# Attention by head quads with block transposes and 64-row tiles, and an MoE over mapped blocks with resident weights

## The chip, the cores and the metric

The kernel runs on one core of a Trainium2 chip. The core has five engines that run side by side: TensorE (PE; its weight loads are listed as PEld), VectorE (DVE), ScalarE (ACT), GpSimd (POOL) and SyncE (SP). DMA queues are started from SP, ACT and POOL. The metric is device time in microseconds (us), from the first instruction to the last with what lies around them; smaller is better. Operands lie in SBUF (128 partitions), TensorE's results in PSUM.

## The reference

```python
# q, k, v: [B=8, H=8, S=576, D=64] f32
scores = q @ k.T / 8 - slope[h] * |i - j|       # slope[h] = 2 ** -(h + 1)
scores = where(0 <= i - j < 128, scores, -1e9)
x = (softmax(scores) @ v).transpose(0, 2, 1, 3).reshape(4608, 512)

y_dense = relu(x @ w1_dense) @ w2_dense         # 512 -> 512 -> 512
logits = x @ w_gate                             # 8 experts
e = argmax(logits, 1); g = softmax(logits)[e]
y_moe[t] = g[t] * (relu(x[t] @ w1[e[t]]) @ w2[e[t]])
out = y_dense + y_moe                           # [4608, 512] f32
```

A row of queries sees at most 128 keys, so a tile of 128 keys meets 256 queries: its own 128 and the next.

## The kernel before, in words

The order of the instructions on each engine is set at compile time by a scheduler that also places the semaphores; the program's order is its guide, and pools with a fixed number of buffers limit how far work runs ahead.

**Start.** The buffer of rows for the MoE, `xs_dram` (8 experts x 1024 slots x 512 bf16), is filled with zeros by 16 DMAs of 512 KB (L147), and a list of gates and token numbers, `meta_dram`, is initialised (L139).

**Attention**, `process_batch` (L336), once per batch, all 8 heads together. q, k (SP's queue) and v (ACT's) come in tiles of 128 rows with runs of 256 bytes. TensorE transposes q and k by head pairs in f32 (L374, L380); ACT copies them out (L385, L391, L397), q into two halves that POOL has filled with zeros (L365, L366), so that one matmul over 128 rows serves two heads. v is split into a bf16 high and low part on DVE (L410, L413). `score_key_tile` takes 4 heads and 128 keys: QK matmuls in f32r (a reduced f32 that runs at one column a cycle here) with K=128 (L438, L455), a matmul that adds the mask (L445, L462), the exponential on ACT (L470), a cast to bf16 `phi` on ACT (L475) and the rest `plo` on DVE (L479). Per query tile and head, 3 matmuls for each of two key tiles give the weighted sum and the row sum (L520). DVE copies it out of PSUM (L529, L532), normalises it (L534, L536) and casts it (L545); TensorE transposes it (L556), ACT copies that (L561).

**Gate**, `gate_group` and `gate_block` (L319, L182), five blocks of tokens per batch: the logits in f32 (L322), then about 25 small DVE operations for each block, with a running total that each block takes from the one before. Two indirect scatters on POOL per block bring the row to its expert's next slot (L301) and gate and token number to `meta_dram` (L312).

**MoE**, from L579: 32 pairs of 128-row blocks, 8 blocks per expert whatever their fill. The weights of an expert come in f32 and are cast on ACT (L607 to L617); the rows come through transposing DMAs (L621); the token numbers through L626 and a cast on DVE (L633). Hidden layers dense and expert (L638, L650: 16 matmuls of 256 columns each), relu on ACT (L646, L658), second layers (L663, L674: 512 columns), DVE adds them with the gate (L671, L682), and POOL scatters the 128 rows to the output (L690); slots without a token have a number out of bounds.

Of the kernel before, what the change touches and what calls it, by code (L numbers as in the profile page):

```python
# [22 lines left out]
def kernel(  # L23
# [44 lines left out]

# [27 lines left out]
    nc.vector.tensor_copy(out=pidx_f, in_=pidx_i)  # L96

    d_i = consts.tile([P, PW], I32, name="d_i")
    nc.gpsimd.iota(d_i, pattern=[[1, PW]], base=0, channel_multiplier=-1)
    d_f = consts.tile([P, PW], F32, name="d_f")  # L100
    nc.vector.tensor_copy(out=d_f, in_=d_i)
    inv = consts.tile([P, PW], F32, name="inv")
    inv2 = consts.tile([P, PW], F32, name="inv2")
    nc.vector.tensor_single_scalar(out=inv, in_=d_f, scalar=0.0, op=ALU.is_lt)
    nc.vector.tensor_single_scalar(
        out=inv2, in_=d_f, scalar=float(WINDOW - 1), op=ALU.is_gt
    )
    nc.vector.tensor_tensor(out=inv, in0=inv, in1=inv2, op=ALU.add)
    big = consts.tile([P, PW], F32, name="big")
    nc.vector.tensor_scalar_mul(out=big, in0=inv, scalar1=NEG_BIG)  # L110
    maskbP = []
    mb_f = consts.tile([P, PW], F32, name="mbf")
    for pi in range(NHP):
        mbp = consts.tile([P, 2, PW], BF16, name=f"mbp{pi}")
        for hh in range(2):
            h = 2 * pi + hh
# [611 lines left out]
```

## Time and profile before

| what | value |
|---|---|
| median of 3 runs | 842.09 us (839.64 to 844.87) |
| profiled execution: span from first to last instruction | 840.9 us |
| busy share PE / DVE / ACT / POOL | 72% / 45% / 40% / 24% |
| mean granted TensorE clock | 0.81 |
| 0 to 85 us | constants, zero fill, first loads |
| 85 to 530 us | attention and gate |
| 530 to 564 us | last gate, scatters, first loads of the MoE |
| 564 to 841 us | MoE, 32 pairs of blocks |

The profile lists the busy time of the engines, the idle time before each group of instructions with the event that ended it, and the time in which DMAs land. The granted clock is the share of 2.4 GHz at which TensorE was let run. The four stages are cut by the trace: the last attention matmul (L520) starts at 529.9 us, the first MoE matmul (L638) at 564.2 us. No time around the span is listed; the median of the runs is 1.2 us more than the span.

### The profile page before, as it was taken

Reading aid. Unit: us, or ns where it says so; the run is one execution under the profiler, and the core shown is the slowest. Engines: PE = TensorE matmul, PEld = TensorE weight load, DVE = VectorE, ACT = ScalarE, POOL = GpSimd, SP = SyncE. Lnnn points to the kernel's source line nnn. Section 1 sums busy time; section 2 is a strip of 40 time slices with the busy share of each in tenths; the row PEclk is TensorE's granted clock in tenths of the full one; section 3 lists DMA queues with packets and bytes.
Section 4 is the critical chain, followed back from the end, with each engine's and each line's share of the span. In section 5 each row is a group of like instructions: output and inputs, shape, how many; then the busy total and the mean of one; then the engine's idle time right before and its main releaser. Section 6 shows DMA issues by size and latency. Waiting matters only on the chain. (4 is left out here: it accounts for less than half of the span.)

```text
span 840.9 us, 12351 instructions
## 1 busy us (share of the span) xinstructions
PE 605.5 (72%) x4478; PEld 401.2 (48%) x4520; DVE 374.6 (45%) x1432; ACT 335.4 (40%) x499; POOL 201.8 (24%) x340
## 2 busy tenths in 40 slices
PE   0047948958857868777778678419798878979894
PEld 0035536545435546456357356216556545555562
DVE  7006545646636547638528635503243323333342
ACT  0037129239138148156166276402423414333221
POOL 6000323322231232332130310121222222222122
PEclk9987558559659568668568587659989999999998
DMA  9999025125125026124233034823536444322320
GB/s 73 265 258 145 13 64 104 24 71 124 28 54 117 22 63 117 47 59 94 64 72 65 20 110 156 258 42 83 145 86 157 136 97 128 95 62 69 88 59 32
DMA packets 190973, 79.14 MB, mean 94 GB/s; under 512 B 170047, under 2 KB 178239, under 8 KB 190912
## 3 DMA queue, kind: packets, MB, share of 16 engines
q1 hardware_dynamic: 136240, 41.06, 25.5%
q10 hardware_dynamic: 46480, 23.07, 10.9%
q0 software_dynamic: 8192, 14.22, 5.2%
q8 instruction: 36, 0.59, 0.4%
q14 instruction: 25, 0.20, 0.1%
HBM read 47.27 MB, written 29.99 MB: 92 GB/s over the span
## 5 line engine op out<-in xcount | busy, mean ns | idle before, releaser
L479 DVE TENSOR_TENSOR plo<-p,phi 128x1024 bf16<-128x1024 f32 (+2 forms) x80 | 79.7, 1005 | 126.8 <-ACT phi L475 125.9
L690 POOL DMA_INDIRECT out_dram<-yout,tok_i x64 | 63.0, 985 | 215.6 <-DVE yout L682 89.1
L520 PE MATMUL ax<-vxh,phi 128*128 128x72 bf16 (+1 forms) x576 | 95.8, 224 | 14.6 <-DVE xsav L532 11.5
L520 PE MATMUL ax<-vxh,plo 128*128 128x72 bf16 (+1 forms) x576 | 93.0, 221 | 12.1 <-DVE plo L479 12.1
L520 PEld LDWEIGHTS <-phi 128*128 128x128 bf16 (+2 forms) x1152 | 81.3, 115 | 33.0 <-DVE xsav L532 13.4
L520 PE MATMUL ax<-vxl,phi 128*128 128x72 bf16 (+1 forms) x576 | 94.2, 221 | 0.0
L646 ACT ACTIVATE hdr<-hd 128x1024 bf16<-128x1024 f32 x32 | 32.7, 1023 | 152.2 <-PE hd L638 152.2
L663 PE MATMUL yd<-w2d,hdr 128*128 128x512 bf16 x241 | 66.4, 392 | 30.7 <-DVE ydsb L671 30.2
L638 PE MATMUL hd<-xst,w1d 128*128 128x256 bf16 x512 | 67.8, 278 | 19.8 <-DMA xst<-xs_dram 19.5
L633 DVE CAST tok_i<-meta 128x2 int32<-128x2 f32 x32 | 5.4, 169 | 167.5 <-DMA out_dram<-yout,tok_i 141.6
L470 ACT ACTIVATE p<-sq 128x1024 f32<-128x1024 f32 (+2 forms) x80 | 67.5, 853 | 20.1 <-PE sq L462 11.7
L520 PEld LDWEIGHTS <-plo 128*128 128x128 bf16 (+1 forms) x576 | 68.1, 120 | 15.2 <-DVE plo L479 14.2
L301 POOL DMA_INDIRECT xs_dram<-xnb,slot_i x40 | 39.5, 988 | 144.3 <-DVE onehot L207 104.9
L475 ACT CAST phi<-p 128x1024 bf16<-128x1024 f32 (+2 forms) x80 | 69.4, 879 | 1.5
L638 PEld LDWEIGHTS <-w1d 128*128 128x128 bf16 x512 | 51.0, 100 | 39.1 <-issue 20.6
L674 PE MATMUL ym<-w2e,hmr 128*128 128x512 bf16 x244 | 67.0, 391 | 1.9 <-ACT hmr L658 0.7
L374 PE MATMUL trq<-ident_f,qf 128*128 128x128 f32 (+1 forms) x160 | 36.4, 371 | 37.1 <-ACT qT L391 25.7
L650 PE MATMUL hm<-xst,w1e 128*128 128x256 bf16 x512 | 61.1, 273 | 0.0
L438 PE MATMUL sq<-qT,kT 128*128 128x512 f32 x96 | 57.1, 648 | 4.7 <-ACT p L470 4.4
L312 POOL DMA_INDIRECT meta_dram<-meta,slot_i x40 | 40.6, 1016 | 77.7 <-DMA meta_dram<-meta,slot_i 45.7
L322 PE MATMUL lt<-xtg,wg_sb 128*8 128x64 f32 (+1 forms) x128 | 52.5, 583 | 3.7 <-ACT xtg L561 3.7
L663 PEld LDWEIGHTS <-hdr 128*128 128x128 bf16 x256 | 25.6, 100 | 58.7 <-issue 37.0
(104 smaller groups left out, 1075.2 us busy)
## 6 DMA issues: line engine op xcount, KB each, us to landing
vf<-in_v_dram ACTq DMA_DIRECT2D x32, 256.0 KB, 3.1
qf<-in_q_dram SPq DMA_DIRECT2D x32, 256.0 KB, 6.3
kf<-in_k_dram SPq DMA_DIRECT2D x32, 256.0 KB, 6.3
w2e_f<-in_moe_w_dram ACTq DMA_DIRECT2D x8, 1024.0 KB, 9.1
w1e_f<-in_moe_w_dram SPq DMA_DIRECT2D x8, 1024.0 KB, 6.7
xs_dram<-zinit ACTq DMA_DIRECT2D x8, 512.0 KB, 9.2
xs_dram<-zinit SPq DMA_DIRECT2D x8, 512.0 KB, 10.8
vf<-in_v_dram ACTq DMA_DIRECT2D x8, 128.0 KB, 5.5
```

The source lines that it names most:

```text
L312: nc.gpsimd.indirect_dma_start(out=meta_dram[:, :], out_offset=bass.IndirectOffsetOnAxis(ap=slot_i[:rows, 0:1], axis=0), in_=meta[:rows, : ...
L322: nc.tensor.matmul(out=lt[:E, :ncols], lhsT=wg_sb[:, ds, :], rhs=xtgrp[:, ds, :ncols], start=(ds == 0), stop=(ds == 3),)
L438: nc.tensor.matmul(out=o_ap, lhsT=kT[:, pi, q0 : q0 + krows], rhs=qT[:, pi, :, q0 : q0 + nq], start=True, stop=False,)
L470: nc.scalar.activation(out=p32[:krows, :, :nq], in_=sq_v[:krows, :, :nq], func=ACT.Exp,)
L475: nc.scalar.copy(out=phi[:krows, hq * 4 : hq * 4 + 4, :nq], in_=p32[:krows, :, :nq],)
L479: nc.vector.tensor_tensor(out=plo[:krows, hq * 4 : hq * 4 + 4, :nq], in0=p32[:krows, :, :nq], in1=phi[:krows, hq * 4 : hq * 4 + 4, :nq], o ...
L520: nc.tensor.matmul(out=ax_slice(h), lhsT=lt_, rhs=rt_, start=(imm == 0), stop=(imm == nmm - 1),)
L638: nc.tensor.matmul(out=hd[:, fc, :], lhsT=w1d[:, kc, fc * P : (fc + 1) * P], rhs=xst[:, kc, :], start=(kc == 0), stop=(kc == 3),)
L650: nc.tensor.matmul(out=hm[:, fc, :], lhsT=w1e[:, kc, fc * P : (fc + 1) * P], rhs=xst[:, kc, :], start=(kc == 0), stop=(kc == 3),)
L663: nc.tensor.matmul(out=yd, lhsT=hdr[:, fc, bi * P : (bi + 1) * P], rhs=w2d[:, fc, :], start=(fc == 0), stop=(fc == 3),)
L674: nc.tensor.matmul(out=ym, lhsT=hmr[:, fc, bi * P : (bi + 1) * P], rhs=w2e[:, fc, :], start=(fc == 0), stop=(fc == 3),)
L690: nc.gpsimd.indirect_dma_start(out=out[:, :], out_offset=bass.IndirectOffsetOnAxis(ap=tok_i[:, bi : bi + 1], axis=0), in_=yout[:, :], in_o ...
```

## The change

The whole kernel is written anew around the same arithmetic (high and low bf16 parts of p and v, f32r for QK, f32 for the logits).

**Attention** works in 16 units of 4 heads, with 5 key tiles each, in one software order (`steps`): scores of step n, attend of step n-2. `load_unit` (L125) brings q and k by one POOL DMA each, [128 partitions, 18 rows x 64] in runs of 4608 bytes. `prep_qk` (L143) has DVE transpose 32x32 blocks, one instruction for q and one for k, and then 16 SBUF-to-SBUF DMAs on SP put the pieces in place. Head pairs lie in 64-row halves, so the QK matmuls have K=64 (L275) and the two halves write two PSUM banks; no zeros are needed. The mask goes first (L266). `phi` is no longer cast: it is the upper half of each f32 of `p32`, read with a stride. `attend` has 24 matmuls of 64 or 65 columns; the normalisation reads PSUM (L330, L332); POOL casts the row (L342). v's high part is made on ACT, its low part on POOL.

**Gate**, `gate(b)` (L371), once per batch for all five blocks: the logits in four column tiles of TensorE, one matmul that adds them, 13 DVE operations, ranks of all blocks from matmuls that accumulate, five scatters of rows that carry gate and token number behind the 512 values (L456).

**Weights**: all 18 matrices are cast to bf16 by POOL's DMA while attention runs (L76) and stay in SBUF.

**MoE**: a table made on DVE (L513 to L589) maps 43 blocks (36 full ones, and up to 7 that the experts' remainders need) to experts. Per block: POOL gathers 128 rows (L602) and makes the token numbers (L611); 4 transposes (L621) and a DVE copy (L625); hidden layers with the weights as the moving operand, 512 columns (L630, L638), the expert's address from a register that TensorE loads (L593); relu on ACT with the gate as its scale (L646, L647); 8 transposes (L651), two DVE copies (L655, L656); dense and expert second layers accumulate in one bank (L659, L667); ACT copies it out (L675); POOL scatters it (L676).

```diff
+            nc.gpsimd.dma_start(
+                out=w_all[:, e, wi, :, :],
+                in_=src.rearrange("(ks p) f -> p ks f", p=P),
+            )
...
-        eng.dma_start(
-            out=xs_dram[zi * 4 * P : (zi + 1) * 4 * P, :].rearrange(
-                "(k p) c -> p k c", p=P
-            ),
-            in_=zinit,
-        )
...
-                nc.gpsimd.memset(qT_f[0:D, pi, 1, :], 0.0)
-                nc.gpsimd.memset(qT_f[D:P, pi, 0, :], 0.0)
...
+            nc.gpsimd.dma_start(
+                out=t.rearrange("p r c d -> p (r c d)"),
+                in_=src[b, hs].rearrange("h (p r) d -> (h p) (r d)", r=R),
+            )
...
+        nc.vector.transpose(
+            out=s.rearrange("p c (x r) -> p r c x", r=R),
+            in_=t.bitcast(F32),
...
+                nc.sync.dma_start(
+                    out=d.bitcast(F32)[hh * D + 32 * c : hh * D + 32 * c + 32, pl, 0:S],
+                    in_=s[32 * g : 32 * g + 32, c, :],
+                )
...
+        for r in range(2):
+            nc.tensor.matmul(
+                out=sq[:, r, 0 : 2 * nq],
+                lhsT=ident_b,
+                rhs=mask[:, hq, r, :, 0:nq],
+                start=True,
+                stop=False,
+            )
+        for pl in range(2):
+            for r in range(2):
+                nc.tensor.matmul(
+                    out=sq[:, r, pl * nq : (pl + 1) * nq],
+                    lhsT=kT[r * D : (r + 1) * D, pl, k0 : k0 + P],
+                    rhs=qT[r * D : (r + 1) * D, pl, k0 : k0 + nq],
+                    start=False,
+                    stop=(pl == 1),
+                )
...
-                    nc.scalar.copy(
-                        out=phi[:krows, hq * 4 : hq * 4 + 4, :nq],
-                        in_=p32[:krows, :, :nq],
-                    )
...
+        phi = p32.bitcast(BF16).rearrange("p r l (c t) -> p r l c t", t=2)[:, :, :, :, 1]
+        plo = ppool.tile([P, 2, 2, PW], BF16, name="plo", tag="plo")
+        nc.vector.tensor_tensor(
+            out=plo[:, :, :, 0:nq],
+            in0=p32[:, :, :, 0:nq],
+            in1=phi[:, :, :, 0:nq],
+            op=ALU.subtract,
...
+            n = 0
+            for kj in kl:
+                phi, plo = pbuf[(u, kj)]
...
+                for lhs, rhs, w in (
+                    (hi, vh[:, kj, g, :], D + 1),
+                    (hi, vl[:, kj, g, :], D),
+                    (lo, vh[:, kj, g, :], D + 1),
+                ):
+                    n += 1
+                    nc.tensor.matmul(
+                        out=ax_v[:rows, g, 0:w],
+                        lhsT=lhs,
+                        rhs=rhs,
...
-                nc.vector.tensor_copy(
-                    out=xs[:rows, 0:7, :], in_=ax[:rows, 0, 0 : 7 * VW]
-                )
-                nc.vector.tensor_copy(out=xs[:rows, 7, :], in_=ax[:rows, 1, 0:VW])
...
+        recip = gs.tile([P, 4], F32, name="recip", tag="recip")
+        nc.vector.reciprocal(out=recip[:rows], in_=ax_v[:rows, :, D])
+        xf = xpool.tile([P, 4, D], F32, name="xf", tag="xf", bufs=4)
+        nc.vector.tensor_tensor(
+            out=xf[:rows],
+            in0=ax_v[:rows, :, 0:D],
+            in1=recip[:rows].unsqueeze(2).to_broadcast([rows, 4, D]),
+            op=ALU.mult,
+        )
...
+            for ds in range(4):
+                nc.tensor.matmul(
+                    out=lp[32 * ds : 32 * ds + 32, 0:HF],
+                    lhsT=wg_pad[:, ds, :],
+                    rhs=xT[:, ds, hf * HF : (hf + 1) * HF],
+                    start=True,
+                    stop=True,
+                )
+            nc.scalar.copy(out=lt[:, hf * HF : (hf + 1) * HF], in_=lp[:, 0:HF])
...
+        pc = psum_m.tile([P, NT + 1, E], F32, name="pc", tag="misc")
+        for t in range(NT):
+            nc.tensor.matmul(
+                out=pc[:, t + 1 : NT + 1, :],
+                lhsT=ones_b,
+                rhs=oh[:, t, :].unsqueeze(1).to_broadcast([P, NT - t, E]),
...
+            rows = min(P, S - t * P)
+            ins = nc.gpsimd.indirect_dma_start(
+                out=xs_dram[:, :],
+                out_offset=bass.IndirectOffsetOnAxis(ap=slot[:rows, t : t + 1], axis=0),
+                in_=xrow_i[:rows, t, :],
+                in_offset=None,
...
+    for n in range(len(steps) + LAG):
+        if n < len(steps):
+            u, kj = steps[n]
+            scores(u, kj)
+            if kj == 0 and u + 1 < NU:
+                prep_qk(u + 1, "k")
...
+            if kj == 3 and u + 2 < NU:
+                load_unit(u + 2)
+            if kj == 4:
+                if u % 2 == 0:
+                    load_weights(E if u == 0 else u // 2 - 1)
+                    if u == NU - 2:
+                        load_weights(E - 1)
+        if n >= LAG:
+            u, qi = steps[n - LAG]
+            attend(u, qi)
+            if qi == NT - 1 and u % HQ == HQ - 1:
+                gate(u // HQ)
...
+            er = nc.values_load(
+                er_i[0:1, j : j + 1],
+                engines=[PEE],
...
+            nc.gpsimd.indirect_dma_start(
+                out=xm_i[:, :],
+                out_offset=None,
+                in_=xs_dram[:, :],
+                in_offset=bass.IndirectOffsetOnAxis(ap=row_i[:, j : j + 1], axis=0),
+                bounds_check=NSLOT - 1,
...
+            nc.gpsimd.tensor_tensor(
+                out=tok_i,
+                in0=xm_i[:, TC : TC + 1],
+                in1=inval_i[:, j : j + 1],
+                op=ALU.add,
...
+            for kc in range(4):
+                nc.tensor.matmul(
+                    out=hm,
+                    lhsT=xT[:, kc, :],
+                    rhs=w_all[:, bass.DynSlice(er, 1), 0, kc, :],
+                    start=(kc == 0),
...
+            nc.scalar.activation(out=hr[:, 0, :], in_=hd, func=ACT.Relu)
+            nc.scalar.activation(out=hr[:, 1, :], in_=hm, func=ACT.Relu, scale=gate)
...
+            for c in range(8):
+                nc.tensor.transpose(
+                    out=hps[:, c, :], in_=hr_f[:, c * P : (c + 1) * P], identity=ident_b
+                )
+            hT = mpool.tile([P, 8, P], BF16, name="hT", tag="hT")
+            nc.vector.tensor_copy(out=hT[:, 0:4, :], in_=hps[:, 0:4, :])
+            nc.vector.tensor_copy(out=hT[:, 4:8, :], in_=hps[:, 4:8, :])
...
+            for c in range(4):
+                nc.tensor.matmul(
+                    out=y,
+                    lhsT=hT[:, 4 + c, :],
+                    rhs=w_all[:, bass.DynSlice(er, 1), 1, c, :],
+                    start=False,
```

**DVE at the end of a batch.** Before: the end of the last query tile's chain, and the first block's gate with the second's beginning in it. `lg` is a block's logits, `totals_f` the running count, `rank` a token's place.

```order
L545 CAST xnb<-xnf 64x512
L188 COPY lg<-ltp 128x8
L190 MAX mx<-lg 128x8
L192 TENSOR_SCALAR negmax<-mx 128x1
L207 TENSOR_SCALAR onehot<-lg,mx 128x8
L216 ISA junk,eidx_f<-onehot,evals_f 128x8
L216 ISA eidx_f 128x1
L281 TENSOR_TENSOR totals_f<-totals_f,pt 1x8
L249 ISA junk,rank<-onehot,pc 128x8
L249 ISA rank 128x1
L285 CAST t_i<-totals_f 1x8
L188 COPY lg<-ltp 128x8
```

After: the end of the second unit of a batch. `ks` and `qs` are the transposed k and q of the next unit, `pc` the counts, `basee` the experts' next slots.

```order
L332 TENSOR_TENSOR xf<-ax,recip 64x256
L146 STREAM_TRANSPOSE ks<-kraw 128x18x64
L396 TENSOR_REDUCE mx<-lg 128x5
L399 TENSOR_TENSOR lgs<-lg,mx 128x40
L403 SCALAR_TENSOR_TENSOR cand<-lgs,em_152 128x40
L407 TENSOR_REDUCE e_1312<-cand 128x5
L444 TENSOR_REDUCE se<-ex 128x5
L410 TENSOR_TENSOR oh<-em_152,e_1312 128x40
```

```order
L431 TENSOR_TENSOR sl<-pc,basee 128x40
L437 TENSOR_TENSOR sl<-sl,oh 128x40
L442 TENSOR_TENSOR basee<-basee,pc 128x8
L439 TENSOR_REDUCE slot_f<-sl 128x5
L441 CAST slot<-slot_f 128x5
L146 STREAM_TRANSPOSE qs<-qraw 128x18x64
L291 TENSOR_TENSOR plo<-p_1194 128x1024
```

One chain serves five blocks now, and the next unit's `ks`, `qs` and first `plo` stand around and behind it.

**TensorE and POOL in the MoE.** Before, TensorE goes from the dense hidden layer to the expert's:

```order
L638 LDWEIGHTS w1d
L638 MATMUL hd<-xst,w1d 128x256
L650 LDWEIGHTS w1e
L650 MATMUL hm<-xst,w1e 128x256
L650 LDWEIGHTS w1e
```

After, at the same place (`y` belongs to the block before, `hd` and `hm` to this one):

```order
L667 MATMUL y<-w_all,hT 128x512
L630 LDWEIGHTS xT
L630 MATMUL hd<-w_all,xT 128x512
L638 LDWEIGHTS xT
L593 TENSOR_LOAD er_i
L638 ISA
L638 MATMUL hm<-w_all,xT 128x512
```

and POOL, after (`xr_79` and so on are five buffers for gathered rows):

```order
L676 DMA out_dram<-yo,tok_i 4608x512
L602 DMA xr_79<-xs_dram,row_i 128x260
L611 TENSOR_TENSOR tok_i<-xr_79,inval_i 128x1
L676 DMA out_dram<-yo,tok_i 4608x512
L602 DMA xr_81<-xs_dram,row_i 128x260
```

Before, POOL had the scatter alone. Now a register load stands between the two hidden layers on TensorE, and each of POOL's scatters stands behind a gather and an addition that reads what that gather brings.

**POOL between the second and the sixth unit.** Before, POOL has memsets and the scatters here; after, the loads of weights stand among the loads of q and k and the casts:

```order
L76 DMA w_all<-in_moe_w_dram 128x4x512
L342 CAST xrow<-xf 128x256
L76 DMA w_all<-in_moe_w_dram 128x4x512
L130 DMA kraw<-in_k_dram 128x1152
L342 CAST xrow<-xf 64x256
L76 DMA w_all<-in_moe_w_dram 128x4x512 x2
L130 DMA qraw<-in_q_dram 128x1152
L76 DMA w_all<-in_moe_w_dram 128x4x512
L168 TENSOR_TENSOR vl<-vf_67,vh_69 128x1280
```

All 18 loads of weights stand in the stretch of POOL's order that ends before the sixth unit's loads.

## Rows read from the trace of the kernel before

**Rows 1.** Page, part 1: busy time, share of the span and instructions.

```profile
PE 605.5 (72%) x4478; PEld 401.2 (48%) x4520; DVE 374.6 (45%) x1432; ACT 335.4 (40%) x499; POOL 201.8 (24%) x340
```

**Rows 2.** Stages: stretch, its length, each engine's busy time, granted clock, DMA share, GB/s.

```profile
30.00:85.00 55.00, 27.34 (x205) 18.81 (x206) 13.87 (x21) 23.59 (x32) 0.91 (x6) 0.85 0.97 235
85.00:530.00 445.00, 337.17 (x2720) 226.09 (x2733) 240.98 (x1095) 217.21 (x375) 113.85 (x217) 0.72 0.31 74
530.00:564.00 34.00, 5.25 (x40) 3.62 (x37) 11.35 (x114) 5.67 (x15) 9.46 (x10) 0.55 0.49 128
564.00:841.00 277.00, 233.59 (x1509) 151.23 (x1536) 92.36 (x160) 87.06 (x76) 63.02 (x64) 0.96 0.38 95
```

**Rows 3.** The same stretch, instructions on tile `ax` alone: PE, DVE.

```profile
85.00:530.00 445.00, 103.97 (x1608) 29.34 (x73) 0.72 0.31 74
```

**Rows 4.** Waits, 0 to 110 us: engine, line, releaser, us in total, times, longest.

```profile
ACT qT L391 <- DMA xs_dram<-zinit: 28.5, 1, 28.5
```

**Rows 5.** Waits, 140 to 520 us.

```profile
ACT ex L197 <- DVE negmax L192: 44.3, 30, 5.3
PE pc L227 <- DVE onehot L207: 36.2, 30, 5.3
```

**Rows 6.** Waits of DVE, 564 to 841 us.

```profile
DVE tok_i L633 <- DMA out_dram<-yout,tok_i: 141.6, 26, 8.2
```

**Rows 7.** Groups by line and shape: busy us, mean ns of one, idle before.

```profile
L479 DVE TENSOR_TENSOR plo<-p,phi 128x1024 bf16<-128x1024 f32 x48 | 57.9, 1221 | 121.2 <-ACT phi L475 120.4
...
L479 DVE TENSOR_TENSOR plo<-p,phi 128x768 bf16<-128x768 f32 x16 | 15.2, 948 | 0.8 <-ACT phi L475 0.8
...
L479 DVE TENSOR_TENSOR plo<-p,phi 64x256 bf16<-64x256 f32 x16 | 6.6, 415 | 4.8 <-ACT phi L475 4.6
...
L534 DVE RECIPROCAL recip<-xsav 128x8 f32<-128x8 f32 x32 | 6.2, 195 | 0.3
...
L118 DVE SCALAR_TENSOR_TENSOR mbf<-d_f,big 128x256 f32<-128x256 f32 x8 | 3.4, 422 | 0.2
```

**Rows 8.** Groups by line and shape, the other engines.

```profile
L322 PE MATMUL lt<-xtg,wg_sb 128*8 128x512 f32 x64 | 44.3, 857 | 0.0
...
L561 ACT COPY xtg<-xtp 128x512 f32<-128x512 f32 x32 | 18.7, 585 | 69.5 <-PE xtp L556 69.5
...
L671 DVE COPY ydsb<-yd 128x512 f32<-128x512 f32 x64 | 43.7, 683 | 13.7 <-PE yd L663 10.2 <-PE hm L650 2.9 <-issue 0.2
...
L520 PEld LDWEIGHTS <-phi 128*128 128x128 bf16 x896 | 58.8, 110 | 10.3 <-ACT phi L475 4.9 <-DVE xsav L532 2.3 <-issue 0.5
...
L663 PE MATMUL yd<-w2d,hdr 128*128 128x512 bf16 x241 | 66.4, 392 | 30.7 <-DVE ydsb L671 30.2
```

**Rows 9.** PE's timeline from 318 us: start, length, instruction.

```profile
318.20 0.26 PE L520 MATMUL ax<-vxl,phi 128*128 128x72 bf16 x1
318.26 0.26 PE L520 MATMUL ax<-vxh,plo 128*128 128x72 bf16 x1
...
321.74 0.39 PE L445 MATMUL sq<-mbp,ident_b 128*128 128x512 bf16 x1
321.96 0.20 PE L520 MATMUL ax<-vxh,phi 128*128 128x72 bf16 x1
321.99 0.20 PE L520 MATMUL ax<-vxl,phi 128*128 128x72 bf16 x1
```

**Rows 10.** SP's timeline from 316 us.

```profile
316.40 0.37 SPq L348 DMA_DIRECT2D kf<-in_k_dram  x1
```

**Rows 11.** Page, parts 3 and 6: a queue's packets, MB, share; issues, KB each, landing.

```profile
q0 software_dynamic: 8192, 14.22, 5.2%
...
qf<-in_q_dram SPq DMA_DIRECT2D x32, 256.0 KB, 6.3
...
w1e_f<-in_moe_w_dram SPq DMA_DIRECT2D x8, 1024.0 KB, 6.7
```

**Rows 12.** Line 690, the MoE's scatter, and POOL's timeline from 644 us.

```profile
L690 POOLq MOVE  x64: 29/29/29, 557.7 to 833.4; - x64
...
DMA to landing us min/median/max: 2.1/2.8/6.4
...
645.14 0.98 POOL L690 DMA_INDIRECT out_dram<-yout,tok_i  x1 [3.07 <-DVE yout L682]
648.68 0.98 POOL L690 DMA_INDIRECT out_dram<-yout,tok_i  x1 [2.55 <-DMA out_dram<-yout,tok_i]
...
836.50 0.98 POOL L690 DMA_INDIRECT out_dram<-yout,tok_i  x1 [1.86 <-DMA out_dram<-yout,tok_i]
```

More of the change, by code (lines that the diff above doesn't have):

```diff
@@ L64, with prep_v @@
+    def prep_v(u):
+        vf = vfs[u % 2]
+        vh = vhs[u % 2]
+        vl = qtp.tile([P, NT, 4, D], BF16, name="vl", tag="vl")
+        nc.scalar.copy(out=vh[:, :, :, 0:D], in_=vf)
+        nc.gpsimd.tensor_tensor(out=vl, in0=vf, in1=vh[:, :, :, 0:D], op=ALU.subtract)
+        vparts[u] = (vh, vl)
+    load_unit(0)
     ident_f = consts.tile([P, P], F32, name="ident_f")
@@ L108 @@
[L108 to L116, printed above, removed]
+    tok_c = consts.tile([P, NT], I32, name="tok_c")
+    nc.gpsimd.iota(tok_c, pattern=[[P, NT]], base=0, channel_multiplier=1)
@@ new lines, with gate @@
+    scat_group = "scatters"
+    def gate(b):
+        xT, xrow = cur["xT"], cur["xrow"]
+        lt = lts[0]
+        HF = S // 2
+        for hf in range(2):
+            lp = psum_m.tile([P, 512], F32, name="lp", tag="misc")
+            for ds in range(4):
[5 more added lines that the diff above has]
+                    stop=True,
+                )
+            nc.scalar.copy(out=lt[:, hf * HF : (hf + 1) * HF], in_=lp[:, 0:HF])
+        lg = psum_m.tile([P, NT, E], F32, name="lg", tag="misc")
+        for t in range(NT):
+            nc.tensor.matmul(
+                out=lg[:, t, :],
+                lhsT=lt[:, t * P : (t + 1) * P],
+                rhs=sel,
@@ L576 @@
-        for b in range(B):
-            process_batch(b)
+            tc.declare_no_dep(
+                ins.ins,
+                group=scat_group,
+                reason="every token has a row of its own",
+            )
+            tc.add_to_no_dep_group(scat_group, ins.ins)
+    steps = [(u, kj) for u in range(NU) for kj in range(NT)]
+    prep_qk(0, "q")
+    prep_qk(0, "k")
+    prep_v(0)
+    load_unit(1)
+    LAG = 2
+    for n in range(len(steps) + LAG):
[4 more added lines that the diff above has]
+                prep_qk(u + 1, "k")
+            if kj == 2 and u + 1 < NU:
+                prep_qk(u + 1, "q")
+                prep_v(u + 1)
+            if kj == 3 and u + 2 < NU:
[10 more added lines that the diff above has]
+                gate(u // HQ)
@@ new lines @@
+        nc.vector.tensor_tensor(
+            out=wt[:, 2, 0 : E - 1], in0=n8[:, 1:E], in1=n8[:, 0 : E - 1], op=ALU.subtract
+        )
+        cb = rt.tile([P, E], F32, name="cb")
+        nc.vector.tensor_copy(out=cb, in_=wt[:, 1, :])
+        for e in range(1, E):
+            nc.vector.tensor_tensor(
+                out=cb[:, e : e + 1],
+                in0=cb[:, e - 1 : e],
+                in1=wt[:, 1, e : e + 1],
+                op=ALU.add,
+            )
+        ge = rt.tile([P, NB, E - 1], F32, name="ge")
```

906 lines of the change are left out of this document (369 added, 537 removed).

## The prediction

> **What bounds the kernel now.** I read the page's shares first, then cut the span into stages, then asked in each stage what ends the waits. TensorE is the busiest engine, but only 72% of the span [rows 1], and the stages have different limits [rows 2]. Up to 85 us little computes: ACT stands 28.5 us behind one of the zero-fill DMAs [rows 4], while the DMA engines are 97% busy at 235 GB/s. From 85 to 530 us TensorE is busy 337 of 445 us, at a granted clock of 0.72. The program has 1728 `ax` matmuls (8 batches x 8 heads x 9 pairs of tiles x 3); 1608 of them fall in this stretch [rows 3], 7.44 of 8 batches, so a batch takes 445/7.44 = 59.8 us. Here the engines wait for each other in the gate: ACT 30 times for `negmax`, 44.3 us, and TensorE 30 times for `onehot`, 36.2 us [rows 5], with DVE's many small operations (195 ns for 8 columns, rows 7) in between. From 530 to 564 us nearly nothing is busy: the last gate and its scatters run alone. From 564 to 841 us the clock is 0.96 and TensorE is busy 234 of 277 us; DVE waits 26 times for a scatter to land [rows 6]. A pair of blocks takes 277/32 = 8.65 us.
>
> **The change part by part**, against the profiled execution's 840.9 us of span plus 1.2 us around it.
>
> *Start, 22 us* until the first scores. Removed are the zero fill and the clogged queue. There remain: some 3 us of POOL's memsets; the landing of q and k, 590 KB each, 6.3 us for 256 KB and 6.7 us for 1024 KB [rows 11], taken 9 for two behind each other; two block transposes; SP's 16 copies at 0.37 us an issue [rows 10], 5.9 us, of which q's lie under k's transpose; and 2.1 us to land [rows 12]. 3 + 9 + 2.8 + 5 + 2.1 = 21.9.
>
> *The block transpose* is not in the trace. Nearest is a DVE operation over f32, 1221 ns for 1024 columns [rows 7]; for 1152 columns that is 1.37 us. Twice that, 2.7, is the upper end; below it 0.7, if one operand instead of two halves it. I take 1.4.
>
> *A unit on DVE.* plo 3 x 1.221 + 0.948 + 0.415 = 5.0; five reciprocals and five normalisations of 256 columns, 5 x (0.195 + 0.422) = 3.1 [rows 7]; two transposes 2.8. Sum 10.9. At the unit's end the last attend, both transposes and the first plo of the next unit stand in one chain, and I add half of the transposes and one normalisation, 2.3 us, for what can't overlap: 13.2. The `xsav` copies, the split of v and the casts are gone from DVE; POOL and ACT do what remains of these, one unit ahead, which costs nothing while POOL isn't held up by its loads.
>
> *A unit on TensorE.* A 512-column matmul starts 0.22 us before the next at full clock [rows 9]. Mask and QK are 2048 columns per full key tile, and the five tiles are worth four full ones (3, 0.75 and 0.25): 4 x 4 x 0.22 = 3.5. Attend: 108 matmuls at 0.033 = 3.6 warm (0.06 cold, rows 9). Ten f32 transposes by a quarter of the 857 ns of an f32 matmul of 512 columns [rows 8]: 2.1. Each step goes from 128-row tiles to 64-row tiles and back; a 512-column matmul is listed with 392 ns and its successor starts after 220 [rows 8, 9], so if each change waits for the rest it costs 0.18 us, ten times a unit, 1.8. Sum 11.0. The Trainium skill, "TensorEngine Tiling (Array Packing)", Key Properties, says that changing the tiling mode drains TensorE. By that rule the 1.8 us stand, and without it the total would be 16 x 1.8 = 29 us lower; no run so far shows a change of mode.
>
> *The gate, once a batch.* TensorE's order has it whole before the next unit's scores. Eight f32 matmuls of 288 columns by the 857 ns row, 3.9; ACT's copy 0.3 [rows 8]; five DVE operations at 0.2 up to `oh`, 1.0; small matmuls 1.1: 6.3 us of chain. The other eight operations run under the next scores.
>
> *A batch, 35 us.* By DVE 2 x 13.2 + 6.3 = 32.7. By TensorE 2 x 11.0 / 0.72 + 5 = 35.6, if the clock stays at 0.72. I take 35, since the waits of the one are not all covered by the other; ends 31 (DVE's 10.9 with half the tail, and the gate) and 42 (transposes at 2.7 and the gate at 9). 8 x 35 = 280.
>
> *The weights, 35 us.* 18 loads of 1 MB at the 235 GB/s that the start reached [rows 2] take 18 x 4.5 = 81 us. All stand in POOL's order ahead of the sixth unit's loads; of the units computed meanwhile four are loaded among them, each 1.77 MB of q, k and v and 1.18 MB of copies, 12.6 us at the same rate, so 131 us of DMA meet the compute of five units, 5 x 17.5 = 87 us. The difference is 44; I take 35, since the weights begin before the first unit is done; ends 0 (the engines move both at once) and 75 (the loads come at half the rate when they share it). ACT's weight casts and their waits in the MoE are gone.
>
> *From the last gate to the MoE, 21 us* (34 before, rows 2): gate 6.3, slots 1, five issues of 1.0, landing 2.8 [rows 12], the first gather 3.5, transposes and copy 1.5, first register load 1. The table on DVE, about 30 small operations of 0.2 us, lies beside the scatters. Ends 18 and 30.
>
> *A block of the MoE, 5.5 us.* TensorE: 16 matmuls at 0.22 = 3.5, twelve transposes of 128 columns at a quarter of that = 0.7; relu on ACT 0.585 and a DVE copy of up to 0.683 [rows 8] stand between, partly under the next block's `hd`: 4.9. POOL: the gather's reader starts 3.54 us after it, as 648.68 after 645.14 [rows 12]; with `tok_i` 0.17 and the scatter's 0.98 a cycle is 4.7, and if the scatter also waits for ACT's copy and one more issue is in the way, 6.3. I take 5.5, the middle of POOL's ends. 43 x 5.5 = 236.5, against 277 now for 32 pairs; ends 4.9 and 6.3, 211 and 271.
>
> *Tail* 4.4 us, as now from the last scatter's start at 836.5 [rows 12], and 1.2 around the span.
>
> Sum: 22 + 35 + 280 + 21 + 236.5 + 4.4 + 1.2 = **600 us**. With all lower ends 505, with all upper ends 740.
>
> **The rivals.**
>
> *TensorE's weight loads set the unit.* `phi` is read with a stride of two, 72 loads a unit. Listed with 110 ns a load now hides behind matmuls that start every 33 ns [rows 8, 9]. If strided loads don't hide, a unit grows by 72 x 0.077 = 5.5 us and the total by 89, to 689. For it: every matmul of attend has its own load. Against: contiguous ones hide fully. 0.17.
>
> *The register load shows in every block.* A MOVE takes 29 ns on POOL, and a small transfer 2.1 us to land [rows 12]. On TensorE the load stands behind the last `hd`, where five matmuls, 1.1 us, may cover it. If 1.0 us is left, 43 blocks give 43, and 643. 0.08. The Trainium skill, "DMA: Bandwidth & Descriptors", Latency and other measured facts, gives about 600 ns as the floor of a tensor_load; by that an estimate of 26 us, 626, if nothing covers it; no run here shows one.
>
> *All goes side by side.* No backlog of weights, units at DVE's own pace, blocks at TensorE's: 505. For it: DMA share is 0.31 in the attention now. Against: every stage now has waits that no busy share shows. 0.14.
>
> *Slower.* POOL's casting loads of q and k become the bound. A unit needs 1.18 MB; what isn't attention is 22 + 21 + 236.5 + 5.6 = 285, so the kernel is slower than before from (842 - 285)/16 = 34.8 us a unit on, 34 GB/s. At 25 GB/s: 47 us a unit, 1040. Nearest is POOL's queue, 8192 packets with 14.22 MB in 5.2% of 16 engines' span: 700 us of engine time, 85 ns for 1736 bytes, 20 GB/s an engine, ten times what is needed. 0.04.
>
> **How the numbers follow.** The forecast, with its terms near the taken values (545 to 655), has 0.55; the weight loads 0.17, the register 0.08, the fast case 0.14, slower 0.04, and 0.02 is left for what I don't see. The prediction is 600. The range of 505 to 720 takes in the fast case's sum, the register and most of the weight-load case; left out are the slow case, sums near all upper ends, and gains beyond every lower end. Faster by over 1% (what a measurement can tell here) 0.95, within 1% 0.01, slower 0.04.
>
> **What would show it.** Right: first scores before 25 us; a batch of 31 to 42 us, with DVE's waits short; q and k of units two to five landing late behind weights, with TensorE idle there; blocks at a steady 5 to 6 us whose scatter on POOL waits behind the gather's landing. Wrong: attend matmuls further apart than 33 ns warm; a block transpose over 2.7 us; POOL's loads at tens of GB/s; TensorE waiting on its sequencer before each `hm`; DMA engines idle while the first units wait.

## The result: 603 us for 842, and the profile after

The changed kernel takes 603.35 us (median of 4 runs, 598.56 to 605.63) against 841.85 us: a ratio of 0.7168 (95% interval 0.713 to 0.7206). 600 was forecast. Ratios, here and below, leave out executions of a slower state of the chip (one each of e5_qk128, e12_pad and the kernel before), while the medians take in all. The profiled execution has a span of 601.4 us. Page, part 1, to be read against [rows 1]:

```profile
PE 456.5 (76%) x3828; PEld 272.7 (45%) x3828; DVE 303.2 (50%) x554; ACT 193.0 (32%) x298; POOL 271.2 (45%) x366
```

The stages, columns as in [rows 2]: the first two batches, five batches, from the last attend to the first MoE matmul, and the MoE.

```profile
24.00:123.00 99.00, 70.18 (x664) 48.96 (x665) 61.28 (x96) 28.88 (x43) 47.66 (x66) 0.69 1.09 227
123.00:335.00 212.00, 157.73 (x1642) 110.35 (x1641) 155.45 (x236) 73.83 (x107) 99.65 (x118) 0.69 0.63 153
361.00:381.00 20.00, 4.27 (x42) 2.61 (x40) 9.13 (x41) 1.88 (x5) 8.78 (x10) 0.61 0.15 44
381.00:602.00 221.00, 201.60 (x1200) 95.06 (x1200) 50.30 (x129) 76.04 (x129) 92.24 (x126) 0.97 0.18 64
```

The stages are cut by these rows of the timelines: the first QK matmul, a batch's first scatter (batches 1, 2 and 7), the last attend, and the `hd` matmuls that open the first and the last block of the MoE.

```profile
24.27 0.94 PE L275 MATMUL sq<-qT,kT 64*128 64x256 f32 x3 [4.11 <-DMA kT<-ks]
...
79.69 1.07 POOL L456 DMA_INDIRECT xs_dram<-xrow,slot  x1 [3.38 <-issue]
...
123.28 1.08 POOL L456 DMA_INDIRECT xs_dram<-xrow,slot  x1 [1.01 <-DVE slot L441]
...
334.03 1.09 POOL L456 DMA_INDIRECT xs_dram<-xrow,slot  x1 [6.42 <-DVE slot L441]
...
361.22 0.20 PE L322 MATMUL ax<-vh,plo 128*64 128x65 bf16 x1
...
381.11 1.89 PE L630 MATMUL hd<-w_all,xT 128*128 128x512 bf16 x4 [0.52 <-DVE xT L625]
...
583.33 0.82 PE L630 MATMUL hd<-w_all,xT 128*128 128x512 bf16 x3
```

Five batches take 334.03 - 123.28 = 210.75 us, 42.2 each, where 59.8 stood before and 35 was forecast. In the MoE 42 blocks lie between the two `hd` rows: (583.33 - 381.11)/42 = 4.81 us a block, where 5.5 was forecast. Thus 600 came out of errors of both signs, which the table sums from the same rows. The last batch's gate lies behind 361 us, in the third line; the forecast counts it twice, in its eight batches and in its 21 us.

| term | forecast | measured |
|---|---|---|
| to the first scores | 22 | 24 |
| weights and eight batches, to the last attend at 361 | 315 | 337 |
| last gate to the first MoE matmul | 21 | 20 |
| MoE and tail | 241 | 220 |

Two groups of DVE, by line and shape, are longer than forecast (read them against [rows 7]; the mean in ns is the last number before the second bar):

```profile
L291 DVE TENSOR_TENSOR plo<-p 128x1024 bf16<-128x1024 f32 x48 | 68.9, 1483 | 2.2 <-ACT p L283 2.2
...
L146 DVE STREAM_TRANSPOSE ks<-kraw 128x1152 f32<-128x1152 f32 x16 | 37.4, 2339 | 6.0 <-DMA kraw<-in_k_dram 5.7
...
L291 DVE TENSOR_TENSOR plo<-p 128x768 bf16<-128x768 f32 x16 | 29.4, 1836 | 11.6 <-ACT p L283 11.6
```

The transpose takes 2.34 us, not 1.4. And `plo`, the operation of [rows 7] but for a strided operand, has grown, at 768 columns to nearly twice its 948 ns. The timelines of DVE and POOL at one place say when:

```profile
228.85 5.82 DVE L291 TENSOR_TENSOR plo<-p 128x1024 bf16<-128x1024 f32 x3
...
229.99 3.60 POOL L168 TENSOR_TENSOR vl<-vf,vh 128x1280 bf16<-128x1280 f32 x1
```

Three `plo` beside POOL's subtraction take 5.82 us, where 3 x 1.221 = 3.66 was forecast.

Two rows of TensorE bear on the forecast as well. Attend's matmuls start 0.05 to 0.06 us apart while the granted clock is 0.50, with the strided `phi` (here under its tile's name, `p`) as with the contiguous `plo`, and about as far apart as before (318.20 and 318.26 in [rows 9]). And the gate's logits take 1.18 us:

```profile
232.27 0.24 PE L322 MATMUL ax<-vh,p 128*128 128x65 bf16 x1
232.32 0.24 PE L322 MATMUL ax<-vl,p 128*128 128x64 bf16 x1
232.38 0.24 PE L322 MATMUL ax<-vh,plo 128*128 128x65 bf16 x1
...
362.53 1.18 PE L378 MATMUL lp<-xT,wg_pad 128*32 128x288 f32 x16
```

### The profile page after: what moved, and what is told of

The parts are those of the page before. It is cut to its first block, busy times and chain, and to the rows that moved or that the text cites. A ratio compares the mean times of both kernels' runs of the same rounds, so it can differ in the third digit from the quotient of the medians.

```text
span 601.4 us, 10655 instructions
## 1 busy us (share of the span) xinstructions
PE 456.5 (76%) x3828; PEld 272.7 (45%) x3828; DVE 303.2 (50%) x554; ACT 193.0 (32%) x298; POOL 271.2 (45%) x366
## 5 line engine op out<-in xcount | busy, mean ns | idle before, releaser
L291 DVE TENSOR_TENSOR plo<-p 128x1024 bf16<-128x1024 f32 (+2 forms) x80 | 108.8, 1398 | 15.2 <-ACT p L283 15.2
L322 PE MATMUL ax<-vh,plo 128*128 128x65 bf16 (+1 forms) x576 | 89.0, 225 | 11.1 <-DVE plo L291 11.1
L625 DVE COPY xT<-xps 128x512 bf16<-128x512 bf16 x43 | 18.2, 423 | 156.2 <-PE xps L621 152.7
L322 PEld LDWEIGHTS <-p 128*128 128x128 bf16 (+1 forms) x1152 | 84.0, 122 | 23.6 <-issue 20.6
L266 PE MATMUL sq<-mask,ident_b 128*128 128x512 bf16 (+2 forms) x160 | 60.8, 478 | 42.0 <-ACT p L283 20.9
L322 PE MATMUL ax<-vh,p 128*128 128x65 bf16 (+1 forms) x576 | 90.4, 226 | 0.0
L322 PE MATMUL ax<-vl,p 128*128 128x64 bf16 (+1 forms) x576 | 89.9, 224 | 0.0
L342 POOL CAST xrow<-xf 128x256 bf16<-128x256 f32 (+1 forms) x80 | 44.4, 559 | 79.8 <-DVE xf L332 79.7
L675 ACT COPY yo<-y 128x512 f32<-128x512 f32 x43 | 25.2, 585 | 131.0 <-PE y L667 124.9
L275 PE MATMUL sq<-qT,kT 64*128 64x256 f32 (+2 forms) x320 | 60.3, 405 | 6.1 <-DMA kT<-ks 4.4
L456 POOL DMA_INDIRECT xs_dram<-xrow,slot x40 | 46.5, 1164 | 33.2 <-DVE slot L441 14.1
L676 POOL DMA_INDIRECT out_dram<-yo,tok_i x43 | 43.6, 1014 | 36.9 <-issue 14.7
L275 PEld LDWEIGHTS sq<-qT,kT 64*128 64x128 f32 x320 | 42.2, 262 | 28.9 <-issue 20.5
L630 PE MATMUL hd<-w_all,xT 128*128 128x512 bf16 x172 | 52.3, 387 | 0.9 <-DVE xT L625 0.5
L168 POOL TENSOR_TENSOR vl<-vf,vh 128x1280 bf16<-128x1280 f32 x16 | 45.7, 2856 | 16.0 <-ACT vh L167 15.9
L602 POOL DMA_INDIRECT xr<-xs_dram,row_i x43 | 43.9, 1021 | 16.0 <-issue 14.7
L638 PE MATMUL hm<-w_all,xT 128*128 x172 | 45.0, 385 | 0.0
L659 PE MATMUL y<-w_all,hT 128*128 128x512 bf16 x172 | 44.1, 379 | 0.5 <-DVE hT L655 0.5
```

The source lines that it names most:

```text
L168: nc.gpsimd.tensor_tensor(out=vl, in0=vf, in1=vh[:, :, :, 0:D], op=ALU.subtract)
L266: nc.tensor.matmul(out=sq[:, r, 0 : 2 * nq], lhsT=ident_b, rhs=mask[:, hq, r, :, 0:nq], start=True, stop=False,)
L275: nc.tensor.matmul(out=sq[:, r, pl * nq : (pl + 1) * nq], lhsT=kT[r * D : (r + 1) * D, pl, k0 : k0 + P], rhs=qT[r * D : (r + 1) * D, pl, k ...
L291: nc.vector.tensor_tensor(out=plo[:, :, :, 0:nq], in0=p32[:, :, :, 0:nq], in1=phi[:, :, :, 0:nq], op=ALU.subtract,)
L322: nc.tensor.matmul(out=ax_v[:rows, g, 0:w], lhsT=lhs, rhs=rhs, start=(n == 1), stop=(n == 3 * len(kl)),)
L342: nc.gpsimd.tensor_copy(out=xrow[:rows, qi, hq * 256 : hq * 256 + 256], in_=xf[:rows].rearrange("p h d -> p (h d)"),)
```

## The experiments

Theory A was that DVE's instructions on the path set a unit, and that the subtraction on POOL slows them; rival B, that TensorE at a clock of 0.69 sets it. Differences are taken from ratios to the kernel before, times 842 us.

| run | median, us | ratio (95% interval) |
|---|---|---|
| e1_no_vlow | 573.95 | 0.6785 (0.6731 to 0.684) |
| e3_vlow_late | 579.93 | 0.6836 (0.6784 to 0.6888) |
| e4_no_ktr | 578.17 | 0.6836 (0.6788 to 0.6885) |
| e9_no_vlmm | 551.97 | 0.6506 (0.6455 to 0.6557) |
| e5_qk128 | 591.91 | 0.698 (0.692 to 0.7041) |
| e6_static | 600.77 | 0.7102 (0.7047 to 0.7157) |
| e7_w_late | 578.31 | 0.6849 (0.6807 to 0.6891) |
| e10_tp_next | 575.39 | 0.682 (0.6777 to 0.6862) |
| e11_all | 551.16 | 0.6538 (0.649 to 0.6587) |
| e12_pad | 540.31 | 0.6361 (0.6305 to 0.6418) |

The same five batches in eight of the profiles, each cut by its own first scatters of batches 2 and 7; columns as in [rows 2]. In this order: the changed kernel, e6_static, e1_no_vlow, e3_vlow_late, e10_tp_next, e5_qk128, e11_all, e12_pad.

```profile
123.28:334.03 210.75, 157.17 (x1640) 110.24 (x1640) 154.20 (x236) 72.58 (x106) 98.68 (x117) 0.69 0.63 153
125.72:330.65 204.93, 156.17 (x1640) 108.29 (x1640) 154.16 (x236) 72.20 (x106) 95.11 (x118) 0.68 0.65 158
124.99:307.86 182.87, 149.06 (x1640) 105.48 (x1640) 131.79 (x236) 72.22 (x106) 65.45 (x107) 0.71 0.71 177
129.29:315.51 186.22, 149.19 (x1640) 104.40 (x1640) 141.28 (x236) 72.77 (x107) 90.12 (x118) 0.74 0.69 172
123.12:308.99 185.87, 154.75 (x1640) 111.44 (x1640) 141.60 (x236) 72.25 (x105) 90.18 (x117) 0.69 0.72 176
125.23:322.48 197.25, 144.25 (x1640) 110.55 (x1640) 152.19 (x236) 71.46 (x107) 96.03 (x118) 0.79 0.67 164
99.82:287.27 187.45, 151.62 (x1620) 113.61 (x1640) 141.52 (x236) 72.51 (x106) 97.51 (x127) 0.68 0.89 201
101.79:283.08 181.29, 137.89 (x1620) 108.57 (x1640) 137.16 (x236) 71.76 (x106) 98.20 (x128) 0.79 0.93 211
```

e6 changes nothing in the attention and takes 5.8 us less than the changed kernel here: so much can lie between two executions, and a batch takes 41 to 42 us.

**e1_no_vlow**, the subtraction left out; the low part is a tile of zeros, written once.

```diff
-        nc.gpsimd.tensor_tensor(out=vl, in0=vf, in1=vh[:, :, :, 0:D], op=ALU.subtract)
+        vl = vls[0]
```

> The subtraction that makes v's low part on POOL (2.86 us, 16 times) is left out; the low part is a tile of zeros, its matmuls stay. Theory A, DVE sets a unit and its plo is slowed while POOL subtracts (80 plo take 108.8 us in the changed kernel, 79.7 in the one before): plo falls back to 5.0 us a unit, 16 x 1.8 = 29 us less, about 575 us. Rival B, TensorE at its granted clock of 0.69 sets the unit and DVE's longer plo lies in waits: within 5 us of 603.

32 us less. The groups of `plo` in this run stand where they stood before the change:

```profile
L292 DVE TENSOR_TENSOR plo<-p 128x1024 bf16<-128x1024 f32 x48 | 55.6, 1206 | 2.2 <-ACT p L284 2.2
...
L292 DVE TENSOR_TENSOR plo<-p 128x768 bf16<-128x768 f32 x16 | 15.2, 952 | 17.8 <-ACT p L284 17.8
...
L292 DVE TENSOR_TENSOR plo<-p 128x1024 bf16<-128x1024 f32 (+2 forms) x80 | 78.1, 1011 | 26.2 <-ACT p L284 26.1
```

In all three forms `plo` takes 78.1 us instead of 108.8 (part 5 of both pages): 31 us, and the kernel gained about as much. The stride with which `phi` is read costs DVE nothing in these two forms (1221 and 948 ns in [rows 7]). That the two sums agree doesn't yet show that each microsecond of `plo` counts; e3 bears on it.

**e3_vlow_late**, the same subtraction, behind POOL's cast of query tile 1. ACT's copy of v's high part stands later in the program with it.

```diff
+            with tc.issue_after(cur["cast"]):
+                nc.gpsimd.tensor_tensor(out=vl, in0=vf, in1=vh[:, :, :, 0:D], op=ALU.subtract)
```

> Same work; the subtraction stands in POOL's order behind the cast of query tile 1, where DVE has little plo left. Theory A: most of what leaving it out gives, 15 to 29 us less, 574 to 588 us. Rival B: within 5 us of 603. A third way: the subtraction now slows the normalisation instead (two operands as well), and nothing is won.

28 us less. DVE's timeline at the same place in a unit, then groups of the whole run:

```profile
242.03 3.47 DVE L295 TENSOR_TENSOR plo<-p 128x1024 bf16<-128x1024 f32 x3
...
L170 POOL TENSOR_TENSOR vl<-vf,vh 128x1280 bf16<-128x1280 f32 x15 | 37.9, 2524 | 7.7 <-ACT vh L167 5.7 <-DMA kT<-ks 2.0
...
L295 DVE TENSOR_TENSOR plo<-p 128x256 bf16<-128x256 f32 x16 | 20.0, 1250 | 4.7 <-ACT p L287 4.7
...
L295 DVE TENSOR_TENSOR plo<-p 128x1024 bf16<-128x1024 f32 (+2 forms) x80 | 94.3, 1214 | 19.9 <-ACT p L287 19.8
```

3.47 us for the three that took 5.82. The 2.35 us between them are nearly one subtraction, 2.52 us here; in the changed kernel that subtraction is listed with 3.60. The Trainium skill, "SBUF — State Buffer", Who interferes with whom, says that a DVE instruction with two SBUF inputs contends with a GpSimd instruction that reads SBUF, and that the ports which they share are an exclusive lock; the trace agrees, since DVE loses nearly one whole subtraction. The prediction had costed `plo` at the rate of a kernel in which POOL had memsets and scatters alone.

But half of the slowdown is still there: `plo` takes 94.3 us, and the form of the last key tile 1250 ns. Half of what e1 took from `plo` gives most of e1's gain, so it matters which `plo` meets the subtraction. TensorE's waits for `xf` fell too (28.1 us between 123 and 335 us in the changed kernel, 13.9 here), and the granted clock of the five batches rose from 0.69 to 0.74 (0.71 in e1). How the gain divides among these is not shown.

**e4_no_ktr**, k's transposes left out.

```diff
+        if nm == "k":
+            s = t.bitcast(F32).rearrange("p r c d -> p (r c d)").rearrange("p (c x) -> p c x", c=2)
```

> The block transposes of k (2.34 us each, 16) are left out: the copies read the loaded tile as it is, so the scores are of other numbers; all other instructions stay. Theory A: 16 x 2.34 = 37 us less, about 566 us. Rival B: under 10 us less.

28 us less by the ratio, 25 by the medians, between the two theories but near A: two thirds to three quarters of what was taken from DVE.

**e9_no_vlmm**, 36 of 108 attend matmuls left out as well.

```diff
-                    (hi, vl[:, kj, g, :], D),
```

> As the run without the subtraction, and the 36 matmuls a unit with v's low part are left out too, so TensorE loses a third of attend. Theory A: the same time as the run without the subtraction, within 5 us. Rival B: 16 x 36 x 0.033 to 0.06 = 19 to 35 us less than that run.

23 us less than e1. Theory A falls as it was put: TensorE's attend is on the path too. DVE's and TensorE's parts follow one another in a unit; the kernel gains when either is cut.

**e10_tp_next**, TensorE's transposes of a tile behind the next tile's attend.

```diff
+        if pend:
+            pend.pop()()
...
+        pend.append(tail)
```

> As the run with the late subtraction, and TensorE transposes a query tile's rows only after the next tile's attend matmuls, so that DVE's reciprocal and normalisation lie beside them; the last tile of a unit as before. Theory, the unit is a chain that passes from engine to engine: of the waits between 123 and 335 us (tp for xf 28 us, recip for ax 34 us) most of the smaller goes, in all 16 units some 35 us, about 545 us. Rival, the busier engine sets the unit: within 5 us of the 580 that the late subtraction gave.

1 us less than e3 by the ratio, 5 by the medians, 30 to 34 short of the 35 that the chain was held to give. TensorE's wait for `xf` between 123 and 335 us did fall, here e3 and then this run:

```profile
PE tp L356 <- DVE xf L336: 13.9, 21, 0.9
```

```profile
PE tp L361 <- DVE xf L339: 7.0, 13, 0.9
```

Two things were wrong. The moved subtraction had already taken half of the 28 us that I counted. And in the same five batches, 186.22 us in e3 and 185.87 here, the granted clock went from 0.74 to 0.69 as TensorE waited less: its busy time grew by 5.6 us. The wait that was filled was no time gained.

**e5_qk128**, QK over 128 rows.

```diff
-                    lhsT=kT[r * D : (r + 1) * D, pl, k0 : k0 + P],
-                    rhs=qT[r * D : (r + 1) * D, pl, k0 : k0 + nq],
+                    lhsT=kT[:, pl, k0 : k0 + P],
+                    rhs=qT[:, pl, k0 : k0 + nq],
```

> The QK matmuls use all 128 rows of q and k instead of 64-row halves (each score is then the sum of two heads'); their number, their 256 columns and their order stay, and TensorE never changes its tile size. If a change of mode costs the 0.18 us that the prediction took, ten times a unit, and TensorE's time is on the path for two thirds of what is taken from it: 29 x 0.65 = 19 us less than 603. Rival: 64-row tiles cost nothing or pairs run side by side: the same time, or slower by up to 4 x 4 x 0.11 x 16 x 0.65 = 18 us.

16 us less by the ratio, 11 by the medians, but not as expected. One step of scores, from the first mask matmul to the attend matmul that follows, in the changed kernel and then in this run. The granted clock is 0.50 in both stretches, the lower of TensorE's two levels (1.2 and 2.4 GHz). The last row of each view is the end of the QK matmuls, cut out by a narrower window:

```profile
167.03 1.01 PE L266 MATMUL sq<-mask,ident_b 128*128 128x512 bf16 x2 [0.96 <-issue]
167.98 0.79 PE L275 MATMUL sq<-qT,kT 64*128 64x256 f32 x4
168.70 0.24 PE L322 MATMUL ax<-vh,p 128*128 128x65 bf16 x1
...
168.36 0.41 PE L275 MATMUL sq<-qT,kT 64*128 64x256 f32 x2
```

```profile
164.42 1.01 PE L266 MATMUL sq<-mask,ident_b 128*128 128x512 bf16 x2 [0.74 <-ACT p L283]
164.87 1.42 PE L275 MATMUL sq<-qT,kT 128*128 128x256 f32 x4
166.09 0.28 PE L322 MATMUL ax<-vh,p 128*128 128x65 bf16 x1
...
165.87 0.41 PE L275 MATMUL sq<-qT,kT 128*128 128x256 f32 x1
```

The step takes 1.67 us in both; at full clock it is 0.96 (from 226.66 us) and 0.91 (from 183.01 us in this run). Two things cancel in the 64-row form. Its QK matmuls run in pairs beside each other: two are listed with the 0.41 us of one over 128 rows. But the change of tile size behind them costs: the attend matmul starts 0.34 us behind the last 64-row pair and 0.22 behind the last 128-row matmul, of 256 columns each. That is 0.12 us for this change, where the prediction took 0.18. Since the whole step takes as long, the pairs earn back what the two changes cost.

So QK's form by itself gives this run nothing at the lower level and little at the upper. What differs is the clock: 0.79 against 0.69 in the five batches, where TensorE's busy time falls from 157.2 to 144.3 us. Whether the clock rose because all rows work or because the tile size stays the same is open. (Changes remain in both kernels: the last query tile and the gate use `128*64` and `128*32`.)

**e6_static**, no register.

```diff
-                    rhs=w_all[:, bass.DynSlice(er, 1), 0, kc, :],
+                    rhs=w_all[:, j // 6, 0, kc, :],
```

> The expert of a block is a fixed number (block // 6, so rows meet other weights than theirs), and TensorE loads no register. Theory: the loads are hidden behind matmuls issued before, within 4 us of 603. Rival, the load shows: its 0.30 us 43 times, 13 us less.

6 us less by the ratio, 3 by the medians; the interval overlaps that of the change, so the times alone don't tell 0 from some 10. The changed kernel's timeline of TensorE does: the expert's matmuls, whose address the load brings, start 0.21 us after the last dense one, as any other matmul.

```profile
484.74 0.38 PE L630 MATMUL hd<-w_all,xT 128*128 128x512 bf16 x1
484.95 1.03 PE L638 MATMUL hm<-w_all,xT 128*128 x4
...
489.54 0.38 PE L630 MATMUL hd<-w_all,xT 128*128 128x512 bf16 x1
```

The load's own row reads `L593 PEldq TENSOR_LOAD <-er_i x43: 295/302/561` ns, and it is hidden. The floor of about 600 ns that the Trainium skill, "DMA: Bandwidth & Descriptors", Latency and other measured facts, gives for a tensor_load does not hold here: the median is half of it.

**e7_w_late**, two loads of weights for every two units.

```diff
+                    with tc.issue_after(cur["cast"]):
+                        load_weights(E if u == 0 else u // 2 - 1)
```

> The loads of weights are spread: each expert's two stand in POOL's order behind the cast of query tile 1 of the unit before which the program names them, so two loads meet two units. Theory: the first four units lose what they waited for the backlog, some 15 us (55 us for the first two units against 42 for later ones), about 588 us. Rival: the DMA engines' work is only moved and nothing changes, or the last weights come late for the MoE: 603 or more.

27 us less. The first scatters of batches 1 and 2 of this run:

```profile
69.20 1.07 POOL L458 DMA_INDIRECT xs_dram<-xrow,slot  x1 [1.06 <-DVE slot L443]
...
110.04 1.05 POOL L458 DMA_INDIRECT xs_dram<-xrow,slot  x1 [1.02 <-DVE slot L443]
```

Batch 2 is 13.2 us earlier than in the changed kernel; that is the backlog, for which 35 was forecast. The profiled executions, 582.6 and 601.4 us, differ by 18.8. The other 5.6 come in the five batches that follow, 205.0 us (from 110.04 to 315.06) against 210.8; but e6, whose attention is the changed kernel's, shows 204.9, so this is no gain that could be told from the scatter of executions. The rest of the 27 lies between executions too.

**e11_all**: e3, e10, e7, and POOL's token numbers behind an older scatter.

```diff
+            after = tc.issue_after(scats[j - NXR]) if j >= NXR else ExitStack()
+            with after:
+              nc.gpsimd.tensor_tensor(
                 out=tok_i,
...
+            scats.append(scat.ins)
```

> The late subtraction, the transposes behind the next tile's attend and the spread weights together, and in the MoE POOL adds a block's token numbers behind the scatter of five blocks before instead of right behind its gather. If the gains add: 575 from the first two, less the 25 that the spread weights gave, less 43 x (4.94 - 4.81) = 5 us if POOL's cycle of 4.94 us sets a block now and TensorE's 4.81 then: 546 to 552 us. Rival: the spread weights' gain was partly the waits that the other two take away as well: 560 to 570.

551, as the gains add. Against e10 it is 24 us less; in the profiled executions 23.3 of 28.2 us lie before the first scatter of batch 2 (123.12 us in e10, 99.82 here). In the MoE the expectation was right in size and wrong in place. In the changed kernel POOL's gathers stand 4.94 us apart here, with the addition waiting for the landing:

```profile
483.51 1.02 POOL L602 DMA_INDIRECT xr<-xs_dram,row_i  x1 [0.30 <-issue]
486.36 0.18 POOL L611 TENSOR_TENSOR tok_i<-xr,inval_i 128x1 int32<-128x1 int32 x1 [1.83 <-DMA xr<-xs_dram,row_i]
...
488.45 1.03 POOL L602 DMA_INDIRECT xr<-xs_dram,row_i  x1 [0.30 <-issue]
```

But TensorE's blocks stand 4.81 us apart all the same, and in e11 (331.69 to 533.54 us for 42 blocks) 4.81 on average: POOL's cycle sets no block. POOL starts five gathers ahead and falls behind, with 5.1 us between gathers on average (396.33 to 575.38 us for 35); this shows once, at the end. ACT's last copy and POOL's last scatter, in the changed kernel and then in e11:

```profile
590.59 0.58 ACT L675 COPY yo<-y 128x512 f32<-128x512 f32 x1 [2.91 <-PE y L667]
597.87 0.98 POOL L676 DMA_INDIRECT out_dram<-yo,tok_i  x1 [4.52 <-issue]
```

```profile
540.57 0.59 ACT L695 COPY yo<-y 128x512 f32<-128x512 f32 x1 [2.91 <-PE y L687]
541.93 0.98 POOL L696 DMA_INDIRECT out_dram<-yo,tok_i  x1 [3.69 <-ACT yo L695]
```

The last scatter stands 7.28 us behind that copy in the first and 1.36 in the second: 5.9 us, near the 5 that were expected. What the last scatter of the changed kernel waits for in its 4.52 us the profile doesn't name.

**e12_pad**: e11 with QK over 128 rows, q in two kept tiles with zeros in the other head's rows.

```diff
+        nc.gpsimd.memset(qT.bitcast(F32)[D:P, 0, :, :], 0.0)
+        nc.gpsimd.memset(qT.bitcast(F32)[0:D, 1, :, :], 0.0)
...
+                    rhs=qT[:, r, pl, k0 : k0 + nq],
```

> As the run with all four, and QK over all 128 rows: q stands in two copies' places with the other head's 64 rows zero (two kept tiles, zeroed once), so the scores are those of one head. Same columns, no change of tile size. If what the run on 128 rows gave (11 us) comes on top: about 11 us less than that run, 535 to 541. Rival: with the other waits gone TensorE is the bound and its clock falls again, no gain.

540 us, 11 less than e11 by the medians and 15 by the ratio: it beats both kernels, 10% below the change. The clock of the five batches is 0.79 against e11's 0.68, as in e5, though half of q's rows hold zeros: the rise doesn't need values in all rows.

## Why the prediction was right, point by point

- *Direction and total*: right, 600 against 603, but the closeness is luck. The batches were put some 50 us too low in all, the weights some 20 too high, the MoE 21 too high.
- *A batch, 35 us*: measured 42.2 (41.0 in e6). Two prices on DVE were too low. "I take 1.4" for a block transpose was inside its bounds: 2.34 us, four a batch, 3.8 us more. The other had no bound at all: `plo`, "3 x 1.221 + 0.948 + 0.415", took 6.8 us a unit (108.8/16), 1.8 more, 3.6 a batch, through POOL's subtraction, which was costed at nothing "while POOL isn't held up by its loads": as POOL's time, not as DVE's. Against them stand the gate's logits, 1.18 us for 3.9. That is some 5 of the 6 to 7 us, but as a sum of busy times it proves nothing: e4 gave two thirds to three quarters of what it took from DVE.
- *Busier engine or chain*: the forecast took 32.7 for DVE and 35.6 for TensorE, and 35 for both together. In the five batches TensorE is busy 157.2/5 = 31.4 and DVE 30.8 us a batch, and a batch takes 42.2. It is the overlap that was put too high: in e1 and e9 the work of either engine counts.
- *A sum*: "half of the transposes and one normalisation, 2.3 us" are 1.4 + 0.6 = 2.0, 0.6 us less a batch.
- *Ten changes of tile size a unit, 1.8 us*: the one that rows show cost 0.12 us at the lower level of the clock (e5), so TensorE does stand at a change of mode, as the rule says that the prediction cites. What the forecast left out is that the halves of QK run beside each other, which pays for it.
- *The weights, 35 us*: 13 us by the second batch in e7, 23 in e11 beside the other changes. The bounds of 0 and 75 held.
- *Gate, and the last gate to the MoE*: 21 forecast, 20 measured.
- *A block, 5.5 us*: 4.81. The step that failed is the choice of the middle of POOL's ends: POOL's cycle, within those ends, sets no block. TensorE's 4.9 was right, and POOL costs some 6 us once, at the end (e11).
- *The rivals*: strided weight loads of `phi` hide (rows at 232.27; at full clock attend's matmuls stand 0.03 us apart, from 360.04 us). The register load is hidden (rows at 484.74). POOL's casting loads kept pace: 0.58 us an issue, and behind 123 us no transpose waits for their landing.
- *The signs*: first scores at 24.27 us, before 25; a batch at the edge of its 31 to 42; no steady blocks of 5 to 6 us behind the gather's landing, but 4.81.

## What to carry to other kernels

An operation moved to an idle engine is free only if it doesn't stand in the way of another's: price what POOL reads from SBUF against DVE's two-operand instructions that run at that moment, and choose which of them it meets; here the place alone gave 28 us, though half of the slowdown stayed. A price from a trace holds for the company in which it was measured. When two engines pass a unit to each other, busy shares of 73 and 75% name no bound; take a little from each and look which time follows. And ask of a slower engine that starts ahead whether it sets the pace or only ends late.

## What the runs showed of the hardware that was not expected

- The DVE transpose of 32x32 f32 blocks takes 2.34 us for 128x1152, 2.03 ns a column, against 1.19 for a two-operand operation on f32 (1221 ns for 1024).
- The granted clock of the same five batches rose from 0.69 to 0.79 with QK over 128 rows (e5), also where half of q's rows are zeros (0.68 to 0.79 from e11 to e12), and fell from 0.74 to 0.69 when TensorE waited less (e10 against e3).
- Two QK matmuls on the two 64-row halves start together; the matmul of 128 rows behind them starts 0.12 us later than behind a QK matmul of 128 rows (e5).
- POOL's gathers, slower than TensorE's blocks (5.1 against 4.81 us), cost 5.9 us once at the end and nothing per block (e11).
- A TENSOR_LOAD of one value takes 0.30 us on TensorE's queue.
